# Stores of h and y issued from ScalarE's queue, with a new search of the instruction order

## The chip, the cores and the metric

The kernel runs on one core of a Trainium2 chip. The metric is the device time of one execution in microseconds; of several runs the median is taken. The core's engines work side by side, each through its own list of instructions in order: TensorE (PE; PEld is its weight load) multiplies matrices, VectorE (DVE), ScalarE (ACT) and GpSimd (POOL) work on elements, and SyncE (SP) only issues transfers. Any engine with a queue for transfers can issue one, and it then waits in its own list until the data are ready.

## What is computed

Attention over 32 heads, then two feed-forward layers on the 2304 tokens, all in float32. The names in the code: h is a layer's first product, g what its activation makes of it, y the layer's second product.

```python
def _attn_ref(q, k, v):                       # q, k, v: (4, 8, 576, 64)
    scores = scale * np.matmul(q, k.transpose(0, 1, 3, 2))
    scores = np.where(mask, scores, -1000000000.0)     # causal by blocks of 64
    attn = softmax(scores)
    return np.matmul(attn, v)

def _moe_ref(x, w_in, w_out):                 # x: (2304, 512), d_ff 2048
    h = x @ w_in
    g = np.where(pos, h, np.where(neg, 0.0, (h + beta) ** 2 / (4.0 * beta)))
    return g @ w_out

def _moe2_ref(x, w_in, w_out):
    h = x @ w_in
    g = np.maximum(0.01 * h, h)
    return g @ w_out
```

## The kernel before

**Stages.** Attention by pairs of heads (scores line 651, transposes 743, values 770) runs together with the first layer's first product (lines 877, 887 and 855). Then come the first layer's y (lines 1191 and 1252), the second layer's h (line 1068) and the second layer's y (line 1252 again), whose result is the output. Operands are split into a high and a low part, so that each product is three matmuls.

**Seven products for eight.** From the first layer's y on, each 2x2 block product is made of seven products (`PRODUCTS`), one PSUM bank or pair of banks each. `sums` (line 970 and on) puts them together: ScalarE copies the first product into an SBUF tile (line 978, the copy), and VectorE adds the other six in seven additions (line 976), each of which frees a bank.

**The second layer's h.** `h_step(b, p, ...)` makes one step: 42 matmuls, the sum into a tile of A0 or A1 in turn, the activation in place (Prelu, line 1072, on ScalarE) and one store of 576 KB into the DRAM array `gd[1]` (line 1073). There are 4 parts b of 288 positions with 8 steps p each, 32 steps in all. The copy of a step can only start when the store of the step two before it, from the same tile, has landed.

**y between the layers.** The first layer's y goes to the DRAM array `x2d`: the first 384 positions by `y_group` (stores in `y_out`, line 1124, 4 of 384 KB), the rest in three units of 256 positions by `y_unit` (line 1260, 4 stores of 256 KB each). In a unit each step p loads g (line 1231, `gd`), VectorE makes sums and differences of it (line 1211), ScalarE rounds them to high parts (lines 1236 and 1237, the conversions) and VectorE subtracts for the low parts (1238 and 1240). The second layer's y runs through `y_unit` too and stores to `out` (line 1268, 18 stores, two for the last unit of 128 positions).

**What sets the order.** Nothing is run by hand: the code above only records operations in a `Plan`, each with an engine, a cost in ns and what it reads and writes. `Plan.schedule` then lists them: it simulates the engines with the recorded costs, lists forward and backward in turn, disturbs the keys at random, and keeps the best of `TRIES` lists; `SEED` starts the random numbers. Each engine's instructions are written out in that order. A transfer is an operation of SyncE whose cost is its bytes by a fixed rate (`dma`), with the fixed delays of the table `DELAY` to those that wait for it:

```python
def dma(nbytes, prio, fn, r, w, lag=0):
    plan.op("SP", nbytes / 330.0, prio, fn, r, w, lag=lag)
```

In the first 20 us products of zeros (line 545) are put where the plan leaves TensorE idle. Before the change every transfer of the kernel is SyncE's, 588 in all.

Of the kernel before, what the change touches and what calls it, by code (L numbers as in the profile page):

```python
# [36 lines left out]
HALF = S // 2  # L37
NPOS = B * HALF
# [28 lines left out]

ENTRY = 105
SLACKS = (0, 800)
SEED, TRIES = 6, 400  # L70
LATEST, DRAWS = 0, 1


# [299 lines left out]
def fused_kernel(ctx, tc, qk, v, w1, w2, out):  # L373
    nc = tc.nc
    w1, w2 = w1.bitcast(I32), w2.bitcast(I32)
    plan = Plan()
# [14 lines left out]
    x2d = dr.tile([128, 4, 2, NPOS], F32, tag="x2d", name="x2d")  # L391
    gd = [dr.tile([NP2, 128, 4, NPOS], F32, tag=f"gd{i}", name=f"gd{i}") for i in range(2)]
# [29 lines left out]
    def dma(nbytes, prio, fn, r, w, lag=0):  # L422
        plan.op("SP", nbytes / 330.0, prio, fn, r, w, lag=lag)


    stack = {"ps": [], "ps2": [], "psr": []}

# [628 lines left out]
    def h_step(b, p, pr, dp, banks_):  # L1056
        h = (A1, A0)[p % 2].reg(0, 1152, shape=lambda ap: ap.rearrange("p (s t) -> p s t", s=4))
        P = {}
        for o, m in enumerate(ORDER):
            li, ri = PRODUCTS[m]  # L1060
            r = RX[b, ri]
            ps = bank(banks_[0])
            banks_.append(banks_.pop(0))
            P[m] = ps, lambda ps=ps: ps.get()[:, 0:HALF]
            for k, (cw, cx) in enumerate(((0, 0), (1, 0), (0, 1))):
                def f(k=k, cw=cw, cx=cx, ps=ps, li=li, r=r):
                    for kc in range(2):
                        nc.tensor.matmul(ps.get()[:, 0:HALF], lhsT=wc(1, p, cw, li, 128 * kc, 128 * kc + 128), rhs=r.get()[:, cx, kc],  # L1068
                                         start=(k == 0 and kc == 0), stop=(k == 2 and kc == 1), skip_group_check=True)
                pe(266, pr + dp * o / 7 + 0.01 * k, f, [WC[1, p][cw][li > 2], (r, (cx, cx + 1))], [ps])  # L1070
        sums(pr - 6, HALF, h, P, lambda o: h.get()[:, (1, 3, 0, 2)[o]], ALU.add)
        act(1152, pr - 6, lambda: nc.scalar.activation(h.get(), h.get(), AF.Prelu, alpha=0.01), [h], [h], sb=True)  # L1072
        dma(589824, pr - 6, lambda: nc.sync.dma_start(gd[1][p, :, :, b * HALF:b * HALF + HALF], h.get()), [h],
            [(f"g1{p}", (b * HALF, b * HALF + HALF))])

    HOMES = [{"gr": ([(P1, 1536), (P1, 2560), (P1, 3584)], [(P1, 0), (P1, 1152), (P1, 2304), (P1, 3456)]),
# [44 lines left out]
    def y_out(Y, o, i, prio):  # L1121
        pos0, n = Y["pos"], Y["n"]
        b = Y["bufs"][i]
        dma(1024 * n, prio, lambda: nc.sync.dma_start(x2d[:, o, :, pos0:pos0 + n], b[1]()), [b[0]], [(f"x2d{o}", (pos0, pos0 + n))])

    def y_sums(Y, grp, first, prio, P):
        n, bufs = Y["n"], Y["bufs"]
# [85 lines left out]
    def y_unit(layer, pos0, n, p0, dp, banks_):  # L1213
# [4 lines left out]
        w = n if wide else 256  # L1218
# [37 lines left out]
        if wide:  # L1256
            yo = A0.reg(0, 2048, shape=lambda ap: ap[:, 0:8 * n].rearrange("p (o t n) -> p o t n", o=4, t=2))
            sums(p1, 2 * n, yo, P, lambda o: yo.get()[:, o], ALU.subtract)
            for o in (0, 3, 2, 1):
                dma(1024 * n, p1 + 1, lambda o=o: nc.sync.dma_start(x2d[:, o, :, pos0:pos0 + n], yo.get()[:, o]), [(yo, (o, o + 1))],  # L1260
                    [(f"x2d{o}", (pos0, pos0 + n))])
            return
        yo = A0.reg(0, 2048, shape=lambda ap: ap[:, 0:1024 * nt].rearrange("p (k t i n) -> p k t i n", k=2, t=nt, i=2))
        sums(p1, 256 * nt, yo, P, lambda o: yo.get()[:, o % 2, :, o // 2], ALU.subtract)
        for k in range(2):
            for t in range(nt):
                for a, m, t0, d in runs(pos0 + 128 * t, 128):
                    dma(2048 * m, p1 + 1, lambda k=k, t=t, a=a - pos0 - 128 * t, m=m, r=t0 + k * d: nc.sync.dma_start(
                        out[r:r + m, :].rearrange("q (i n) -> q i n", i=2), yo.get()[a:a + m, k, t]), [(yo, (k, k + 1)), (yo, (2 + k, 3 + k))], [])


# [151 lines left out]
```

## Time and profile before

| what | value |
|---|---|
| median of three runs | 934.44 us |
| the three runs | 928.88, 934.44, 935.6 us |
| the profiled execution's own time | 928.28 us |
| span in its profile | 926.5 us |
| TensorE busy | 915.6 us, 99% |
| VectorE, ScalarE, GpSimd busy | 727.7, 519.6, 293.9 us |
| moved by DMA | 216.72 MB |

The span runs from the first to the last instruction in the profile; the time of the execution has a little around it. A busy share is an average over the stages, and a row of a timeline joins neighbouring instructions of one line: its first number is the start, the second the length, both in us, and a bracket at its end gives the idle time ahead of it and what ended that. Landing times of transfers and the waits of SyncE come from views of their own.

### The profile page before, as it was taken

To read this page: it belongs to the slowest core of one execution; us is meant where nothing else is said; L and a number is where in the kernel's file an instruction comes from. 1 tells how busy PE (TensorE), PEld (TensorE's weight loads), DVE (VectorE), ACT (ScalarE), POOL (GpSimd) and SP (SyncE) were. 2 spreads that over 40 slices of the span, in tenths; PEclk is the share of its full clock that TensorE was granted. 3 is DMA by queue.
4 is the path that set the end of the run, shared out by engine and by line. 5 is a ranking of instruction groups with operands and counts; after the bars stand their busy time and mean duration, and the time that the engine had idled before them with its cause. 6 is when DMAs were issued, how large, how long until landed. Compare 5 with 4: busy or idle time off the path is not lost.

```text
span 926.5 us, 18684 instructions
## 1 busy us (share of the span) xinstructions
PE 915.6 (99%) x6818; PEld 827.7 (89%) x6818; DVE 727.7 (79%) x1247; ACT 519.6 (56%) x1014; POOL 293.9 (32%) x490
## 2 busy tenths in 40 slices
PE   9999999999999999999999999999999999999998
PEld 6687887876777878899999999999999999999998
DVE  6998677777777646559989798677879899888977
ACT  7788677787777666653434343344535664434333
POOL 5577787787665400000000040146445000000000
PEclk9999999999999999999999999999999999999999
DMA  8678788788799789656525499987887983544433
GB/s 310 212 224 249 236 281 285 261 275 272 273 315 323 276 263 325 191 172 209 154 84 161 140 348 337 346 290 269 266 279 242 328 269 91 176 132 139 148 91 115
DMA packets 164892, 216.72 MB, mean 234 GB/s; under 512 B 9920, under 2 KB 138432, under 8 KB 164800
## 3 DMA queue, kind: packets, MB, share of 16 engines
q1 hardware_dynamic: 164800, 215.52, 71.8%
q8 instruction: 54, 0.88, 0.4%
q14 instruction: 38, 0.31, 0.1%
HBM read 134.74 MB, written 80.74 MB: 233 GB/s over the span
## 4 chain that ended last, share of the span: by engine, by line
PE 92%; DVE 2%; DMA 2%; ACT 1%; issue 1%; POOL 1%; SPq 0%; POOLq 0%; DVEq 0%; ACTq 0%
PE bank L1252 31%; PE bank L1068 15%; PE bank L855 14%; PE bank L887 7%; PE bank L1191 6%; PE slot L651 5%; PE slot L770 5%; PE slot L743 5%; DMA rg<-gd 1%; DVE ra L976 1%; DMA wcd<-rg 1%; DMA rb<-x1d 1%; ACT rp L573 1%; PE bank L545 1%; PE slot L762 0%
## 5 line engine op out<-in xcount | busy, mean ns | idle before, releaser
L1068 PE MATMUL bank<-rp,w 128*128 128x288 f32 x1344 | 179.7, 294 | 1.2 <-ACT ra L978 0.9
L1068 PEld LDWEIGHTS bank<-rp,w 128*128 128x128 f32 x1344 | 178.1, 188 | 1.8 <-ACT ra L978 1.2
L976 DVE TENSOR_TENSOR ra<-ra,bank 128x288 f32<-128x288 f32 (+2 forms) x280 | 125.8, 488 | 43.7 <-ACT ra L978 21.8
L1252 PE MATMUL bank<-w,rp 128*128 128x256 f32 x1014 | 145.9, 277 | 0.0
L1252 PEld LDWEIGHTS bank<-w,rp 128*128 128x128 f32 x1014 | 129.8, 188 | 0.0
L855 PE MATMUL bank<-ra,w 128*128 128x512 f32 x384 | 100.0, 398 | 0.3 <-DVE rg L838 0.3
L1237 ACT ACTIVATE rp<-ra 128x1024 fp32r<-128x1024 f32 (+1 forms) x48 | 47.5, 991 | 72.5 <-DVE ra L1211 62.7
L855 PEld LDWEIGHTS bank<-ra,w 128*128 128x128 f32 x384 | 70.1, 188 | 17.1 <-issue 2.3
L838 DVE SCALAR_TENSOR_TENSOR rg<-bank,rg 128x512 f32<-128x512 f32 x72 | 49.3, 684 | 38.0 <-ACT rg L837 35.1
L1072 ACT ACTIVATE ra<-ra 128x1152 f32<-128x1152 f32 x32 | 37.3, 1167 | 71.4 <-DVE ra L976 71.4
L1252 PE MATMUL bank<-rp,w 128*128 128x256 f32 x508 | 76.6, 279 | 0.0
L936 POOL TENSOR_TENSOR w<-w 128x128 f32<-128x128 f32 x128 | 66.9, 543 | 26.7 <-DVE w L932 24.7
L1003 POOL TENSOR_TENSOR xs<-xs,rp 128x576 f32<-128x576 f32 x1 | 1.5, 1547 | 212.0 <-DMA xs<-x2d 212.0
L836 ACT ACTIVATE rg<-bank 128x512 f32<-128x512 f32 x72 | 43.1, 598 | 43.2 <-PE bank L855 36.6
L1252 PEld LDWEIGHTS bank<-rp,w 128*128 128x128 f32 x508 | 67.2, 188 | 0.0
L1240 DVE TENSOR_TENSOR rb<-ra,rp 128x1024 fp32r<-128x1024 f32 (+1 forms) x48 | 54.3, 1133 | 3.9 <-ACT rp L1237 0.7
L1252 PE MATMUL bank<-w,rb 128*128 128x256 f32 x294 | 57.0, 277 | 0.0
L887 PE MATMUL bank<-ra,w 128*128 128x256 f32 x352 | 53.6, 289 | 0.0
L855 PE MATMUL bank<-rb,w 128*128 128x512 f32 x192 | 53.1, 398 | 0.0
L887 PEld LDWEIGHTS bank<-ra,w 128*128 128x128 f32 x352 | 45.1, 188 | 3.5 <-issue 2.6
L1252 PE MATMUL bank<-rg,w 128*128 128x256 f32 x280 | 47.7, 279 | 0.0
L1236 ACT ACTIVATE rp<-rp 128x768 fp32r<-128x768 f32 (+1 forms) x33 | 26.4, 803 | 36.2 <-DMA rp<-gd 21.5
(169 smaller groups left out, 1977.6 us busy)
## 6 DMA issues: line engine op xcount, KB each, us to landing
rp<-gd SPq DMA_DIRECT2D x41, 512.0 KB, 4.2
wcd<-w SPq DMA_DIRECT2D x43, 448.0 KB, 4.6
gd<-ra SPq DMA_DIRECT2D x32, 576.0 KB, 4.8
gd<-rg SPq DMA_DIRECT2D x64, 256.0 KB, 3.6
w<-wcd SPq DMA_DIRECT2D x32, 512.0 KB, 5.7
w<-wcd SPq DMA_DIRECT2D x32, 384.0 KB, 5.7
w<-w SPq DMA_DIRECT2D x44, 256.0 KB, 4.6
w<-w SPq DMA_DIRECT2D x16, 512.0 KB, 5.1
```

The costliest lines, as they stand in the source:

```text
L651: nc.tensor.matmul(out, lhsT=x.get()[r, q:q + 128], rhs=x.get()[r, k0 + ka:k0 + kb], start=start, stop=True, skip_group_check=True)
L743: nc.tensor.transpose(s.get()[:, hd, o:o + 128], prob(hd, a, a + 128), ident.get())
L838: dve(512, pv, lambda: nc.vector.scalar_tensor_tensor(gt.get(), ps.get(), 1.0, gt.get(), op0=ALU.max, op1=ALU.min), [ps, gt], [gt])
L855: nc.tensor.matmul(ps.get(), lhsT=win(fc, c, kc), rhs=xview(xt, x, kc), start=(k == 0 and kc == 0), stop=(k == 2 and kc == NKC - 1), skip_ ...
L887: nc.tensor.matmul(ps.get()[:, 256 - j * 256:512 - j * 256], lhsT=win(fc, c, kc), rhs=xview(xt, x, kc), start=(k == 0 and kc == 0 and j == 0),
L936: plan.op("POOL", 430, prio, lambda o=o, a=a, b=b, op=op: nc.gpsimd.tensor_tensor(sl(o), sl(a), sl(b), op=op), [(fx, (a, a + 1)), (fx, (b, ...
L976: dve(cols, prio, lambda: nc.vector.tensor_tensor(out(o), out(a), P[b][1](), op=op), [P[b][0], (slots, (a, a + 1))], [(slots, (o, o + 1))])
L1068: nc.tensor.matmul(ps.get()[:, 0:HALF], lhsT=wc(1, p, cw, li, 128 * kc, 128 * kc + 128), rhs=r.get()[:, cx, kc], start=(k == 0 and kc == 0 ...
L1191: nc.tensor.matmul(ps[t].get()[:, 0:n], lhsT=wc(z, p, cw, li, 128 * t, 128 * t + 128), rhs=x.get()[:, n * zi:n * zi + n], start=(p == 0 an ...
L1237: act(4 * n, pv, lambda tt=tt, ht=ht: nc.scalar.activation(s_(ht, 0, 4), s_(tt, 0, 4), AF.Copy), [tt], [ht], sb=True)
L1240: dve(4 * n, pv, lambda tt=tt, ht=ht, lt=lt: nc.vector.tensor_tensor(s_(lt, 0, 4), s_(tt, 0, 4), bc(s_(ht, 0, 4)), op=ALU.subtract), [tt, ...
L1252: nc.tensor.matmul(ps.get()[:, 256 * t:256 * t + w], lhsT=b if wide else g, rhs=g if wide else b, start=(p == 0 and k == 0 and t == 0), st ...
```

## The change

Stores of three places, and the second of the last two output stores, are recorded as operations of ScalarE. There the plan counts them with 500 ns of ScalarE's time, and their bytes as a delay behind it instead of as SyncE's time. `SEED` goes from 6 to 1, so the search for the order starts from other random numbers.

```diff
-SEED, TRIES = 6, 400
+SEED, TRIES = 1, 400
...
+    def act_dma(nbytes, prio, fn, r, w):
+        plan.op("ACT", 500, prio, fn, r, w, lag=nbytes / 330.0 + 2300)
+
...
-        dma(589824, pr - 6, lambda: nc.sync.dma_start(gd[1][p, :, :, b * HALF:b * HALF + HALF], h.get()), [h],
+        act_dma(589824, pr - 6, lambda: nc.scalar.dma_start(gd[1][p, :, :, b * HALF:b * HALF + HALF], h.get()), [h],
...
-        dma(1024 * n, prio, lambda: nc.sync.dma_start(x2d[:, o, :, pos0:pos0 + n], b[1]()), [b[0]], [(f"x2d{o}", (pos0, pos0 + n))])
+        act_dma(1024 * n, prio, lambda: nc.scalar.dma_start(x2d[:, o, :, pos0:pos0 + n], b[1]()), [b[0]], [(f"x2d{o}", (pos0, pos0 + n))])
...
-                dma(1024 * n, p1 + 1, lambda o=o: nc.sync.dma_start(x2d[:, o, :, pos0:pos0 + n], yo.get()[:, o]), [(yo, (o, o + 1))],
+                act_dma(1024 * n, p1 + 1, lambda o=o: nc.scalar.dma_start(x2d[:, o, :, pos0:pos0 + n], yo.get()[:, o]), [(yo, (o, o + 1))],
...
+                    put, eng = (act_dma, nc.scalar) if k and pos0 + n == NPOS else (dma, nc.sync)
```

Lines of the new file are three higher than before from line 426 on (four from the output store on), so the copy of line 978 is line 981 there, the Prelu 1075, the store of h 1076, the conversions 1239 and 1240, the y store 1263.

**ScalarE, early in the steps of h.** Copies (978, 981), Prelus in place (1072, 1075) and the splitting of inputs (1007, 1010); ra0 and ra1 are the two tiles of h. First before, then now.

```order
L1072 ACTIVATE ra1_7_6070<-ra1_7_6070 128x1152
L978 ACTIVATE ra0_4_4067<-bank4_90 128x288
L1072 ACTIVATE ra0_4_4067<-ra0_4_4067 128x1152
L978 ACTIVATE ra1_7_6070<-bank1_4043 128x288
L1007 ACTIVATE rp1_2_3911<-ra1_7_6070 128x576
L1072 ACTIVATE ra1_7_6070<-ra1_7_6070 128x1152
```

```order
L1075 ACTIVATE ra0_4_4070<-ra0_4_4070 128x1152
L981 ACTIVATE ra1_7_6090<-bank5_91 128x288
L1076 DMA gd1_71<-ra0_4_4070 512x1x288
L1075 ACTIVATE ra1_7_6090<-ra1_7_6090 128x1152
L1076 DMA gd1_71<-ra1_7_6090 512x1x288
L981 ACTIVATE ra0_4_4070<-bank4_90 128x288
```

The stores, which stood in SyncE's list, now stand in ScalarE's: some behind the next step's copy, as the first one here, some straight ahead of it, as the second.

**ScalarE, at the end of the first y unit.** The copy of the unit's first product (978, 981), the stores into x2d (1263), and the conversions of the next unit's g (1236 and 1237; 1239 and 1240). First before, then now.

```order
L1236 ACTIVATE rp2_2_3954<-rp1_2_3911 128x768
L978 ACTIVATE ra0_4_4067<-bank4_90 128x512
L1237 ACTIVATE rp2_2_3954<-ra1_5_4810 128x1024
L1236 ACTIVATE rp2_2_3954<-rp1_2_3911 128x768
L1237 ACTIVATE rg_2_4729<-ra1_5_4810 128x1024
```

```order
L1240 ACTIVATE rg_2_4728<-ra1_5_4806 128x1024
L981 ACTIVATE ra0_4_4070<-bank4_90 128x512
L1263 DMA x2d_69<-ra0_4_4070 128x2x256
L1239 ACTIVATE rg_2_4728<-rp1_2_3930 128x768
L1263 DMA x2d_69<-ra0_4_4070 128x2x256 x3
L1240 ACTIVATE rp2_2_3966<-ra1_5_4806 128x1024
```

One conversion moved ahead of the copy, and three stores stand together ahead of another.

**ScalarE, in the last steps of h.** The copies of the seventh and of the eighth step of the last part (banks 1 and 0), with weight splits (963, 966) and the first conversions of the last y between them. First before, then now.

```order
L1072 ACTIVATE ra0_4_4067<-ra0_4_4067 128x1152
L1237 ACTIVATE rp2_2_3954<-xs_1_237 128x1024
L978 ACTIVATE ra1_7_6070<-bank1_4043 128x288
L963 ACTIVATE w3_1_565<-w2_1_415 128x1024
L963 ACTIVATE w3_1_565<-w2_1_415 128x768
L1236 ACTIVATE rp2_2_3954<-rb0_20_7623 128x768
L963 ACTIVATE w5_1_781<-w4_1_638 128x1024
L1072 ACTIVATE ra1_7_6070<-ra1_7_6070 128x1152
L978 ACTIVATE ra0_4_4067<-bank0_4042 128x288
```

```order
L981 ACTIVATE ra1_7_6090<-bank1_3988 128x288
L1075 ACTIVATE ra0_4_4070<-ra0_4_4070 128x1152
L1076 DMA gd1_71<-ra0_4_4070 512x1x288
L966 ACTIVATE w3_1_616<-w2_1_460 128x1024
L966 ACTIVATE w3_1_616<-w2_1_460 128x768
L1240 ACTIVATE rp2_2_3966<-xs_1_233 128x1024
L1075 ACTIVATE ra1_7_6090<-ra1_7_6090 128x1152
L1239 ACTIVATE rp2_2_3966<-rb0_20_7613 128x768
L1076 DMA gd1_71<-ra1_7_6090 512x1x288
L981 ACTIVATE ra0_4_4070<-bank0_3987 128x288
```

The copy of the seventh step (bank1) stands ahead of a Prelu now, that of the eighth (bank0) behind a Prelu, a conversion and a store.

## Rows read from the trace of the kernel before

**Rows 1.** The page: busy time of each engine; the costliest conversion line

```profile
PE 915.6 (99%) x6818; PEld 827.7 (89%) x6818; DVE 727.7 (79%) x1247; ACT 519.6 (56%) x1014; POOL 293.9 (32%) x490
...
L1236 ACT ACTIVATE rp<-rp 128x768 fp32r<-128x768 f32 (+1 forms) x33 | 26.4, 803 | 36.2 <-DMA rp<-gd 21.5
```

**Rows 2.** Busy us per stretch: PE, PEld, DVE, ACT, POOL; clock, DMA share, GB/s

```profile
0.00:50.00 50.00, 46.17 (x358) 34.20 (x358) 40.76 (x87) 38.50 (x119) 28.55 (x64) 1.00 0.78 256
50.00:397.00 347.00, 344.77 (x2282) 269.83 (x2281) 246.21 (x435) 253.81 (x617) 194.40 (x331) 1.00 0.83 271
397.00:573.00 176.00, 176.00 (x1342) 175.83 (x1343) 146.88 (x198) 71.88 (x78) 9.64 (x4) 1.00 0.62 196
573.00:752.00 179.00, 177.81 (x1342) 177.17 (x1342) 145.19 (x295) 85.09 (x118) 61.30 (x92) 1.00 0.87 288
752.00:926.50 174.50, 170.89 (x1502) 170.69 (x1500) 148.69 (x236) 70.36 (x84) 0.00 (x0) 1.00 0.45 137
```

**Rows 3.** Waits of PE: us in total, times, longest

```profile
PE bank L545 <- DVE wz L541: 1.1, 1, 1.1
...
PE bank L1068 <- ACT ra L978: 0.9, 1, 0.9
...
PE bank L1068 <- DVE ra L976: 0.3, 1, 0.3
```

**Rows 4.** Timeline of the end, VectorE

```profile
922.93 0.42 DVE L976 TENSOR_TENSOR ra<-ra,bank 128x256 f32<-128x256 f32 x1 [0.40 <-PE bank L1252]
```

**Rows 5.** Issues of lines 1073 and 1260: duration ns min/median/max, first and last start

```profile
L1073 SPq DMA_DIRECT2D gd<-ra x32: 518/519/561, 578.5 to 757.1; - x32
...
L1260 SPq DMA_DIRECT2D x2d<-ra x12: 359/362/1322, 488.1 to 574.2; - x12
```

**Rows 6.** Waits of SyncE: us in total, times, longest

```profile
SPq L1231 <- PE bank L1252: 163.9, 50, 10.2
...
SPq L1073 <- ACT ra L978: 31.7, 15, 4.8
SPq L1073 <- ACT ra L1072: 26.2, 13, 3.3
```

**Rows 7.** Waits of ScalarE and VectorE: us in total, times, longest

```profile
ACT ra L1072 <- DVE ra L976: 71.4, 28, 4.8
ACT rp L1237 <- DVE ra L1211: 62.7, 41, 5.0
...
DVE ra L976 <- ACT ra L978: 21.8, 13, 5.0
```

**Rows 8.** Timeline at the end of the first y unit

```profile
485.92 0.60 ACT L978 ACTIVATE ra<-bank 128x512 f32<-128x512 f32 x1 [1.27 <-PE bank L1252]
486.56 3.49 DVE L976 TENSOR_TENSOR ra<-ra,bank 128x512 f32<-128x512 f32 x5 [0.91 <-ACT ra L978]
...
493.56 1.06 ACT L1237 ACTIVATE rg<-ra 128x1024 fp32r<-128x1024 f32 x1 [2.03 <-DVE ra L1211]
...
495.14 0.36 SPq L1260 DMA_DIRECT2D x2d<-ra  x1
```

**Rows 9.** Timeline of the passage from h to the last y

```profile
745.00 1.06 PE L1068 MATMUL bank<-rp,w 128*128 128x288 f32 x6 [0.92 <-ACT ra L978]
...
750.70 0.39 ACT L978 ACTIVATE ra<-bank 128x288 f32<-128x288 f32 x1
...
752.03 0.86 PE L1252 MATMUL bank<-w,rg 128*128 128x256 f32 x6
```

**Rows 10.** Timeline of PE in attention

```profile
202.30 1.08 PE L855 MATMUL bank<-ra,w 128*128 128x512 f32 x4
203.31 0.81 PE L651 MATMUL slot<-w 64*128 64x320 f32 x4
...
206.42 1.08 PE L855 MATMUL bank<-rb,w 128*128 128x512 f32 x4
207.34 2.13 PE L743 MATMUL slot<-ident,w 128*128 128x128 f32 x18
```

More of the change, by code (lines that the diff above doesn't have):

```diff
@@ L1267, in y_unit @@
                 for a, m, t0, d in runs(pos0 + 128 * t, 128):
-                    dma(2048 * m, p1 + 1, lambda k=k, t=t, a=a - pos0 - 128 * t, m=m, r=t0 + k * d: nc.sync.dma_start(
+                    put, eng = (act_dma, nc.scalar) if k and pos0 + n == NPOS else (dma, nc.sync)
+                    put(2048 * m, p1 + 1, lambda eng=eng, k=k, t=t, a=a - pos0 - 128 * t, m=m, r=t0 + k * d: eng.dma_start(
                         out[r:r + m, :].rearrange("q (i n) -> q i n", i=2), yo.get()[a:a + m, k, t]), [(yo, (k, k + 1)), (yo, (2 + k, 3 + k))], [])
```

## The prediction

> **What bounds the kernel now.** First the page's busy shares: TensorE is busy 915.6 of 926.5 us, VectorE 79%, ScalarE 56% [rows 1]. So whatever the change does, it can only work on the 10.9 us in which TensorE is idle, or make TensorE idle more. Next the busy time by stage shows where those 10.9 us lie, at a granted clock of 1.00 throughout [rows 2]: 50.00 - 46.17 = 3.8 us in the first 50 us, 2.2 us in the rest of attention and of the first product, nothing at all in the 176 us of the first layer's y (397 to 573), 1.2 us in the second layer's h and its passage to the last y (573 to 752), and 3.6 us in the last stretch. Then the list of what TensorE waited for: it has twelve rows, three of which the sum uses [rows 3]. All twelve name ScalarE, VectorE, GpSimd or issue; none names a DMA. That is the first thing to see: the change takes stores off SyncE's queue, and TensorE never waited directly for anything that this queue brought.
>
> Of the 10.9 us some can't go: 1.1 us at the start is the wait for the first zeros [rows 3], and the last 3.6 us are the last sum and its store: the last addition starts at 922.93 us, for it waited for TensorE's last product [rows 4], and the rest up to 926.5 is that addition, a store's issue and its landing. So 10.9 - 1.1 - 3.6 = 6.2 us is all that a perfect order could win.
>
> **The change, part by part.** The profiled execution took 928.28 us (span 926.5 and 1.8 around it); the sum is made against that.
>
> *SyncE loses 49 issues*: 32 stores of h, 12 and 4 of y, 1 of the output. An h store holds SyncE 0.52 us, a y store 0.36 us [rows 5], so about 32 x 0.52 + 17 x 0.36 = 23 us of SyncE's time go. What SyncE did there was mostly to wait: 31.7 + 26.2 us for h, but 163.9 us for TensorE to free the buffers of the gd loads [rows 6]. Loads that stood behind an h store can go earlier now. As no idle time of TensorE ended with a DMA [rows 3], I take 0; the bound on the good side is the 6.2 us above, if loads are what makes ScalarE's conversions, and through them TensorE, late.
>
> The Trainium skill speaks here (DMA: Bandwidth & Descriptors, Issuing engines are not separate DMA queues): transfers issued from different engines share the same 16 DMA engines, so issuing from more of them saves only the sequencer's issue time. By that rule this part is worth at most the 23 us of SyncE, none of it on the path, and the sum stays as it is; were a second queue new bandwidth, the stage at a DMA share of 0.87 [rows 2] would be relieved by it, and rival 2 below would be the likelier.
>
> *ScalarE gains the same 49 issues.* No row shows a DMA issued by ScalarE; SyncE's 0.52 and 0.36 us are the nearest, so ScalarE goes from 519.6 to about 543 us, 59%. In the stretch of h it is busy 85.1 of 179 us [rows 2] and gets 17 more. Its idle time covers that: the Prelu waited 71.4 us in 28 waits for the additions, 2.5 us each, and the y conversions 62.7 us for VectorE [rows 7]. What the mean does not cover is order. In the built order 10 of the 32 stores stand straight between their Prelu and the copy that starts the next step's sum, which comes 0.52 us later there. But VectorE already waited 21.8 us for these copies, in 13 waits [rows 7], and TensorE lost only 0.9 us to it [rows 3]: in this stage late copies are absorbed by the other banks. I take 0; the bound on the bad side is 10 x 0.52 = 5.2 us. If that cover is gone, TensorE waits for the bank of the next step's first product.
>
> *At the ends of the first layer's y units* ScalarE now waits in its queue for VectorE's additions. In the trace of before the copy starts at 485.92 and the last store leaves at 495.14, 9 us later; the conversion that is now queued behind the stores started at 493.56, after an idle 2.03 us [rows 8]. The new VectorE order puts the additions closer: five, which took 3.49 us at 486.56, then a subtraction, an addition, a subtraction of half the columns and the last addition, estimated at a fifth of the 3.49 for the same columns: 3.49 + 3.5 x 0.70 = 5.9 us, from 0.64 us after the copy's start as at 486.56. With the last store's issue the held conversion can start 0.64 + 5.9 + 0.36 = 6.9 us after the copy, against 493.56 - 485.92 = 7.6 us. I take 0, the bounds being 0 and 2 us (as long as the idle time there) for each of the three units, 6 us.
>
> *The passage from h to the last y.* In before TensorE stood idle for 0.92 us until 745.00, for the copy of the seventh step of the last part [rows 9], which ScalarE did only after a Prelu and a conversion, and a little later 0.3 us for an addition [rows 3]; together 1.2 us. In the new order that copy stands ahead of the Prelu: this stall should go. The copy of the eighth step, on the other hand, now stands behind a Prelu, a conversion of 768 columns (0.8 us by the page's own mean for that line [rows 1]) and a store (0.5 us), where before it followed its Prelu directly, so it is 1.3 us later. In before it ended at 750.70 + 0.39 = 751.09, and TensorE next used the bank at 752.03 [rows 9]: a margin of 0.9 us, so 0.4 us of the delay shows. -1.2 + 0.4 = -0.8 us; bounds -1.2, and +1.3 if the margin has gone.
>
> *The order searched anew.* Same products, same number of zero products in the start. But counted in the built order TensorE now goes 61 times from products on the full array into those on part of it (lines 651, 762, 770; three more in the new file), 55 before. One such entry costs 0.09 us: four products of 512 columns followed by line 743 take 207.34 - 206.42 = 0.92 us, followed by line 651 203.31 - 202.30 = 1.01 us [rows 10]. 6 x 0.09 = +0.5 us. The start (2.7 us of idle beside the 1.1) is ordered nearly as before; I take 0 there, between -2.7 and +2.7.
>
> *The last output store* leaves from ScalarE as soon as the addition ends; the unit's other store has left SyncE by then. 0, at best -0.4.
>
> Sum: 928.28 + 0.5 - 0.8 = 928.0 us, for an execution like the profiled one. The executions of before lie at 928.28, 928.88, 934.44 and 935.6; nothing in one trace tells why. Their middle, 931.7, is 3.4 above the profiled one, and a median of new runs can fall in either pair; so 928.0 + 3.4 = **931.4 us**.
>
> **The rivals.**
> 1. *No part of it is felt* (the forecast): 931.4, and anything between 925.1 and 943.8, which is 1% either side of 934.44 and about what a measurement of this kernel can tell from no change.
> 2. *Faster: late loads were behind ScalarE's lateness.* The stores no longer hold up loads on SyncE, and the 6.2 us go: 928.28 + 0.5 - 6.2 = 922.6, or 926.0 with the 3.4. For it: 57.9 us of SyncE's waits are for h stores [rows 6]. Against: 2.7 of the 6.2 us lie in the first 50 us and 2.2 more before 397 us [rows 2], where no store is moved.
> 3. *Slower: ScalarE held at a store.* Place: the three ends of y units, where three stores stand together ahead of a conversion. If the additions come later than the order supposes, that conversion and then TensorE wait. It decides once the last addition is more than the 2.03 us late that ScalarE idled there [rows 8]. Price: the 6 us of the units, and with the 5.2 us of the copies 11.2: 928.0 + 11.2 = 939.2, or 942.6 with the 3.4. For it: VectorE took over 9 us for its additions in before. Against: TensorE had no idle time at all there [rows 2], and ScalarE waits for VectorE anyway.
> 4. *Slower a little: stores and loads now run side by side.* At the stage's 196 GB/s [rows 2] a y store of 256 KB takes 1.3 us of all DMA engines (an estimate from that row); a gd load that ScalarE waits for would land up to that much later, at twelve stores 16 us, of which at a quarter on the path 4: 928.0 + 4 + 3.4 = 935.4. The Trainium skill says (DMA: Bandwidth & Descriptors, Queues, rings and completion order) that a DMA engine takes its queue rows in turn, a packet at a time; by that rule a store no longer queues with the loads but shares with them. No run here shows it yet.
>
> **How the numbers follow.** Chances: forecast 0.62, faster rival 0.15, held ScalarE 0.13, side by side 0.10. The range reaches from 922 (the faster rival without the 3.4) to 941 (most of the held case), about 0.8 of the chance. Faster by over 1% means under 925.1: over half of rival 2 and a little of the forecast, 0.12. Slower by over 1% means over 943.8: a third to half of rival 3, and a start that went badly, 0.10. Within 1%: 0.78.
>
> **What would show it.** Right: TensorE busy within 1 us of 915.6 + 0.5; its idle time between 397 and 573 still under 1 us; ScalarE's issue of an h store near 0.52 us; the stall at about 744 us gone or smaller; ScalarE's wait for the additions shorter by the issue time. Wrong: DMA rows among TensorE's waits (rival 4); rows of lines 1252 or 1068 (1255, 1071 in the new file) with idle time ended by ScalarE's conversions or copies, above all near 490, 530 and 572 us (rival 3); store issues on ScalarE of 1 us and more; or more idle time in the first 50 us, which would be the search's doing and not the stores'.

## The result, and the profile after

The changed kernel takes 941.48 us (median of 12 runs, 936.94 to 949.81) against 928.68 for the kernel before beside it: 1.0144 times as long, 95% interval 1.0118 to 1.0169. It is slower, by more than 1%, and it lies just above the forecast range. The profiled execution took 939.9 us, span 938.0.

The stretches of [rows 2] in the changed kernel (busy us of PE, PEld, DVE, ACT, POOL; granted clock, DMA share, GB/s):

```profile
50.00:397.00 347.00, 346.41 (x2285) 271.22 (x2285) 246.19 (x436) 253.82 (x619) 197.78 (x331) 1.00 0.84 272
397.00:573.00 176.00, 176.00 (x1343) 175.84 (x1342) 147.72 (x198) 71.56 (x76) 7.88 (x4) 1.00 0.62 196
573.00:752.00 179.00, 171.25 (x1265) 168.84 (x1264) 132.09 (x277) 77.55 (x108) 63.16 (x92) 0.99 0.80 269
752.00:938.00 186.00, 180.94 (x1576) 180.06 (x1575) 160.28 (x254) 78.38 (x94) 0.00 (x0) 1.00 0.48 146
```

Up to 573 us nothing is lost; TensorE is busy all of 397:573, so the ends of the y units cost nothing. In 573:752, the second layer's h, it does 1265 matmuls where it did 1342. What TensorE (565 to 790 us), ScalarE (565 to 760) and SyncE (556 to 610) waited for (total us, times, longest), from a list of each:

```profile
PE bank L1071 <- ACT ra L981: 4.2, 5, 1.6
PE bank L1071 <- DVE ra L979: 3.4, 3, 2.0
```
```profile
ACT ra L1075 <- DVE ra L979: 34.0, 22, 4.3
ACT ra L981 <- DMA gd<-ra: 24.8, 10, 4.8
...
ACT ra L981 <- DMA x2d<-ra: 8.1, 1, 8.1
```
```profile
SPq L963 <- DMA gd<-ra: 7.3, 1, 7.3
```

In before the Prelu waited 71.4 us for the additions [rows 7], now 34.0. In its place the copy (L981) waits, 24.8 + 8.1 us, for a store to land. Where it begins, on ScalarE's timeline (start, length, what; brackets: idle ahead and what ended it):

```profile
573.44 0.41 ACT L981 ACTIVATE ra<-bank 128x288 f32<-128x288 f32 x1 [1.41 <-PE bank L1255]
574.30 0.37 ACTq L1263 DMA_DIRECT2D x2d<-ra  x1
581.98 0.41 ACT L981 ACTIVATE ra<-bank 128x288 f32<-128x288 f32 x1 [8.12 <-DMA x2d<-ra]
582.28 1.16 ACT L1075 ACTIVATE ra<-ra 128x1152 f32<-128x1152 f32 x1
583.47 0.59 ACTq L1076 DMA_DIRECT2D gd<-ra  x1
587.65 1.17 ACT L1075 ACTIVATE ra<-ra 128x1152 f32<-128x1152 f32 x1 [4.21 <-DVE ra L979]
591.14 0.41 ACT L981 ACTIVATE ra<-bank 128x288 f32<-128x288 f32 x1 [2.33 <-DMA gd<-ra]
591.23 0.57 ACTq L1076 DMA_DIRECT2D gd<-ra  x1
```

The last y store leaves at 574.30. The copy of the second h step uses its tile and stands in ScalarE's list ahead of the first step's Prelu; it can start at 581.98, so the Prelu waits too, and the first h store leaves at 583.47 (578.5 in before [rows 5]). The third copy waits for that landing until 591.14, and the second store behind it, ready at 588.82, leaves at 591.23. TensorE stops twice, and its granted clock falls after the first stop (columns as above):

```profile
578.00:580.00 2.00, 2.00 (x17) 2.00 (x16) 0.45 (x2) 0.00 (x0) 0.00 (x0) 1.00 1.07 399
580.00:582.00 2.00, 0.96 (x8) 0.73 (x6) 0.00 (x0) 0.02 (x1) 0.00 (x0) 1.00 1.06 388
582.00:584.00 2.00, 1.07 (x4) 1.07 (x5) 0.46 (x1) 1.44 (x2) 0.00 (x0) 0.74 0.99 341
584.00:586.00 2.00, 2.00 (x11) 2.00 (x10) 1.64 (x4) 0.00 (x0) 0.00 (x0) 0.50 0.93 292
586.00:588.00 2.00, 2.00 (x15) 2.00 (x15) 1.00 (x3) 0.35 (x1) 0.65 (x1) 0.90 0.89 271
```

**Where the time is, for all runs.** The h products are 1344 matmuls in every run. The table counts from the trace's matmul records how long their stage takes, from the first of them to the last, in its four parts of eight steps (the first holds some 30 us of y's last products too), and what is left from there to the end of the span. That remainder is near 174.6 us in some traces and near 180 in others whose last stage has the same instructions (before and e12); so the h stage tells more than a median does. Only one execution of each kernel was traced. "Places" are those that the h tiles use in turn.

| kernel | h stores issued by | places | median us | ratio to before (95%) | h stage us: parts, sum | rest |
|---|---|---|---|---|---|---|
| before | SyncE | 2 | 928.68 | | 72.2, 44.4, 44.4, 47.6: 208.7 | 174.6 |
| changed | ScalarE | 2 | 941.48 | 1.0144 (1.0118-1.0169) | 79.0, 45.5, 45.7, 49.0: 219.2 | 175.4 |
| *order of before* | | | | | | |
| e16, y stores alone | SyncE | 2 | 928.82 | 1.0007 (0.9985-1.0029) | 72.5, 44.4, 44.4, 47.6: 209.0 | 174.7 |
| e13, behind the Prelu | ScalarE | 2 | 940.27 | 1.0131 (1.0084-1.0177) | 77.3, 44.4, 46.0, 52.1: 219.8 | 174.6 |
| e14, the same | ScalarE | 3 | 933.55 | 1.0062 (1.0042-1.0083) | 72.3, 44.4, 45.2, 50.3: 212.2 | 180.6 |
| e17, e13 with SyncE's wait | ScalarE | 2 | 933.21 | 1.0038 (1.0014-1.0062) | 72.3, 44.4, 44.9, 52.0: 213.7 | 174.6 |
| e15, behind the next copy | ScalarE | 2 | 934.38 | 1.0073 (1.0045-1.0101) | 78.6, 44.4, 44.4, 47.8: 215.3 | 180.3 |
| e18, the same | ScalarE | 3 | 929.40 | 1.0014 (0.9986-1.0041) | 72.6, 44.4, 44.4, 47.6: 209.1 | 175.9 |
| e9, ScalarE busier | SyncE | 2 | 930.07 | 0.9999 (0.9981-1.0018) | 73.0, 44.4, 44.4, 50.0: 211.8 | 174.4 |
| e12 | SyncE | 3 | 928.68 | 0.9996 (0.9967-1.0026) | 72.2, 44.4, 44.4, 47.6: 208.7 | 180.4 |
| *order of the change* | | | | | | |
| e1, all stores SyncE's | SyncE | 2 | 936.81 | 1.0076 (1.0046-1.0106) | 74.7, 44.4, 45.2, 47.5: 211.8 | 179.6 |
| e2, y stores SyncE's | ScalarE | 2 | 943.31 | 1.0128 (1.0079-1.0177) | 78.3, 44.4, 47.9, 49.9: 220.4 | 181.4 |
| e3, wait by VectorE | ScalarE | 2 | 949.45 | 1.0193 (1.0144-1.0242) | 78.4, 44.4, 50.0, 51.0: 223.9 | 180.4 |
| e4 | ScalarE | 3 | 927.69 | 0.9991 (0.9962-1.0020) | 71.5, 44.4, 44.4, 46.5: 206.9 | 174.5 |
| e5, copies behind stores | ScalarE | 2 | 953.40 | 1.0259 (1.0235-1.0284) | 75.6, 50.6, 48.1, 53.8: 228.1 | 180.0 |
| e10, the same | ScalarE | 3 | 944.57 | 1.0165 (1.0119-1.0212) | 74.1, 49.1, 48.4, 52.1: 223.8 | 180.9 |
| *searched anew* | | | | | | |
| e7, seed 1 | SyncE | 2 | 931.91 | 1.0020 (0.9988-1.0052) | 71.7, 44.4, 45.5, 45.8: 207.4 | 174.7 |
| e8, seed 6 | ScalarE | 2 | 945.67 | 1.0188 (1.0158-1.0217) | 83.7, 45.1, 45.4, 48.0: 222.2 | 178.7 |
| e6, later landing | ScalarE | 2 | 956.37 | 1.0289 (1.0262-1.0317) | 75.0, 45.6, 47.4, 55.9: 224.0 | 179.3 |
| e11, plan knows 3 | ScalarE | 3 | 945.68 | 1.0166 (1.0135-1.0198) | 81.8, 45.7, 44.7, 55.7: 227.9 | 172.7 |

Of the 11.5 us between the two spans (938.0 - 926.5), 219.2 - 208.7 = 10.5 lie in the h stage. TensorE idles there for 8.4 us, 1.2 in before; the clock behind the first stop costs some 1.7 us more, an estimate from the rows above (2 us each at 0.74, 0.50 and 0.90).

### The profile page after: what moved, and what is told of

The parts are those of the page before. It is cut to its first block, busy times and chain, and to the rows that moved or that the text cites. A ratio compares the mean times of both kernels' runs of the same rounds, so it can differ in the third digit from the quotient of the medians.

```text
span 938.0 us, 18643 instructions
## 1 busy us (share of the span) xinstructions
PE 921.1 (98%) x6818; PEld 829.8 (88%) x6818; DVE 725.5 (77%) x1247; ACT 519.6 (55%) x1014; POOL 299.5 (32%) x490
## 4 chain that ended last, share of the span: by engine, by line
PE 87%; DMA 6%; DVE 3%; ACT 2%; issue 1%; ACTq 0%; DVEq 0%
PE bank L1255 30%; PE bank L858 14%; PE bank L1071 12%; PE bank L890 7%; PE bank L1194 6%; PE slot L654 6%; PE slot L773 5%; PE slot L746 5%; DMA gd<-ra 5%; DVE ra L979 1%; DMA x2d<-ra 1%; ACT ra L1075 1%; PE bank L548 1%; ACT rp L576 0%; ACT ra L981 0%
## 5 line engine op out<-in xcount | busy, mean ns | idle before, releaser
L1071 PE MATMUL bank<-rp,w 128*128 128x288 f32 x1344 | 184.1, 296 | 7.8 <-ACT ra L981 4.2
L1255 PE MATMUL bank<-w,rp 128*128 128x256 f32 x1014 | 143.5, 276 | 0.7 <-ACT rp L1239 0.6
L1240 ACT ACTIVATE rp<-ra 128x1024 fp32r<-128x1024 f32 (+1 forms) x48 | 47.5, 990 | 70.5 <-DVE ra L1214 69.4
L939 POOL TENSOR_TENSOR w<-w 128x128 f32<-128x128 f32 x128 | 64.4, 522 | 25.0 <-DVE w L935 22.9
L1255 PE MATMUL bank<-w,rb 128*128 128x256 f32 x294 | 55.1, 276 | 0.0
L981 ACT ACTIVATE ra<-bank 128x288 f32<-128x288 f32 (+2 forms) x40 | 17.6, 439 | 65.9 <-DMA gd<-ra 24.8
L890 PEld LDWEIGHTS bank<-ra,w 128*128 128x128 f32 x352 | 45.7, 188 | 5.8 <-issue 5.4
```

Of the source, the lines that this page charges most:

```text
L890: nc.tensor.matmul(ps.get()[:, 256 - j * 256:512 - j * 256], lhsT=win(fc, c, kc), rhs=xview(xt, x, kc), start=(k == 0 and kc == 0 and j == 0),
L939: plan.op("POOL", 430, prio, lambda o=o, a=a, b=b, op=op: nc.gpsimd.tensor_tensor(sl(o), sl(a), sl(b), op=op), [(fx, (a, a + 1)), (fx, (b, ...
L1240: act(4 * n, pv, lambda tt=tt, ht=ht: nc.scalar.activation(s_(ht, 0, 4), s_(tt, 0, 4), AF.Copy), [tt], [ht], sb=True)
L1255: nc.tensor.matmul(ps.get()[:, 256 * t:256 * t + w], lhsT=b if wide else g, rhs=g if wide else b, start=(p == 0 and k == 0 and t == 0), st ...
```

## The experiments

They are told by question; numbers not shown again stand in the table. The expectations call their theories by letters. A: weight loads run ahead of the stores, and these land late. B: copies that stand ahead in ScalarE's list hold up the Prelu and the store behind them. C: the search drew a worse order (in e3's expectation: a second queue lands late by itself). D: the 0.52 us of a store's issue have no room in the chain of a step.

### Seed or stores?

`SEED` alone, in both kernels:

```diff
-SEED, TRIES = 6, 400      # e7: the kernel before
+SEED, TRIES = 1, 400
-SEED, TRIES = 1, 400      # e8: the changed kernel
+SEED, TRIES = 6, 400
```

> The kernel before (all stores SyncE's) with only the seed of the search changed from 6 to 1, as the change has it. Theory C (the new order is a worse draw of the search, and the queue matters little): 935 to 942. Theories A and B (it takes the moved stores): 927 to 932.

> The changed kernel (stores on ScalarE's queue) with the seed of the kernel before, 6. Theory C: 927 to 932. Theory A (landing on the second queue too late for two tiles): 936 to 943. Theory B allows either: the time goes by how many copies stand ahead of the Prelu or store of the step before, over 936 with ten or more, under 932 with three or fewer.

With SyncE's stores the other seed makes no difference that can be told; with ScalarE's stores both seeds lose. As the whole cause theory C falls: it takes the moved stores. What the order of the change costs without them is e1's question, below.

### Which stores?

In the order of the kernel before, one part alone:

```diff
-            dma(... nc.sync.dma_start(x2d[...], yo.get()[:, o]) ...)      # e16, and y_out
+            dma(... nc.scalar.dma_start(x2d[...], yo.get()[:, o]) ...)
-   act(1152, ..., lambda: nc.scalar.activation(h.get(), ... Prelu))      # e13
+   act(1152, ..., lambda: (nc.scalar.activation(h.get(), ... Prelu), nc.scalar.dma_start(gd[1][...], h.get())))
-   dma(589824, ..., lambda: nc.sync.dma_start(gd[1][...], h.get()), ...)
+   dma(589824, ..., lambda: None, ...)
```

> The kernel before with its own order, and the other part of the change alone: the 16 y stores are issued by ScalarE, the h stores stay with SyncE. Theory A as first put (weight loads run ahead once SyncE doesn't wait for y's data): landings of the last y stores over 6 us, a slip of the first h steps, 932 to 938. If only the h stores cost: 927 to 932.

> The kernel before with its own order, and one part of the change alone: the 32 h stores are issued by ScalarE, each right behind its Prelu. The y stores stay with SyncE. Theory D (the issue of 0.52 us in the chain of a step): 8 to 17 us slower, 937 to 946, the h stage longer in each of its four parts. Theory A (late landings on a second queue with two tiles): slower mainly in the first part, at 574:605, 933 to 940. If neither, the time stays at 927 to 932.

The y stores cost nothing. With the h stores alone moved the kernel takes 940.27 us, as much as with the whole change. Moving only the y stores of the changed kernel back to SyncE agrees:

```diff
-  act_dma(... nc.scalar.dma_start(x2d[...], yo.get()[:, o]) ...)        # e2
+  act_dma(... nc.sync.dma_start(x2d[...], yo.get()[:, o]) ...)
```

> The changed kernel, same order, with only the 12 y stores of the three units (line 1263) issued by SyncE again; the 32 h stores stay with ScalarE. Theory A: the weight loads are held up again while y's last unit ends, the store that landed after 7.58 us lands after 4 to 5, the first slip of some 8 us at 574:582 shrinks to under 5, and the time is 931 to 936, part of the loss. Theory B: no change, 937 to 941.

No gain, though the last y store landed after 5.1 us by the trace, 7.6 in the changed kernel: so theory A was wrong on where it starts.

### Is it the landing?

A third place for the h tiles in turn takes the copy's wait for a landing away. A0 grows by 832 columns for it; the order stays.

```diff
-    (("ra0", 2048), ...
+    (("ra0", 2880), ...
+        own, z = ((A1, 0), (A0, 1728), (A0, 0))[(8 * b + p) % 3]      # in h_step; the view is made from here
```

> The changed kernel, same order and queues, but the h tiles go round three places of SBUF in place of two, so that a copy of line 981 waits for the store of the step three before it, not two, and the second step doesn't use the tile of y's last stores. Landings stay late (6 to 8 us) in every theory. Theories A and B both have the loss pass through the copy's wait for a landing: those waits of ScalarE fall from 33 us to under 5, PE is busy over 24 of the 25 us of 573:598, and the time is 928 to 933. If the loss comes by another way (VectorE's order, ScalarE's issues of 0.52 us each), the time stays at 938 to 942.

> The kernel before, its order and SyncE's stores, with three places for the h tiles in turn at the same instructions. A control: only 6 of its 30 copies start right at a landing, so the third place is worth at most 3 us here if it mends what the change broke (925 to 930); if a third place makes any kernel of this kind some 10 us faster, 916 to 922.

> As the run before it (order of the kernel before, the h stores issued by ScalarE right behind the Prelu), with three places for the h tiles in turn, so that no copy waits for a landing. Theory D: as slow as with two places, 937 to 946. Theory A: 927 to 932.

The changed kernel is back at 927.69. The stretch where it lost most, and the landings of its h stores:

```profile
573.00:598.00 25.00, 25.00 (x191) 25.00 (x190) 17.75 (x38) 8.21 (x12) 6.29 (x10) 1.00 1.06 378
```
```profile
DMA to landing us min/median/max: 3.3/5.3/8.7
```

For the changed kernel with two places the same stretch reads

```profile
573.00:598.00 25.00, 21.45 (x149) 20.98 (x148) 11.98 (x27) 6.27 (x9) 2.61 (x5) 0.93 0.89 308
```

The landings are as late as they were: over all 32 stores 3.3/4.9/7.8 us in the changed kernel, and for the first four 8.27, 6.99, 8.45 and 8.70 us with three places, 7.59, 5.75, 7.85 and 5.49 with two. (Over all 32, before has 3.4/4.8/7.9: its landings are shorter at the start of the stage only.) The control e12 gains nothing: the third place mends what the change broke. So the loss of the changed kernel passes through the copies that wait for a landing. In the order of before, with the store straight behind the Prelu, the third place mends the first part (77.3 to 72.3) and 6.7 us of the time, and 933.55 is left: there is a second cause.

### Why do the stores land late?

In e13 the first four h stores land after 9.78, 6.85, 9.02 and 6.70 us, in before after 4.72, 3.91, 5.48 and 4.80. SyncE's timeline in before, then in e13, there with ScalarE's row of the store:

```profile
575.61 0.41 SPq L960 DMA_DIRECT2D w<-wcd  x1
576.08 0.49 SPq L957 DMA_DIRECT2D w<-wcd  x1
578.48 0.56 SPq L1073 DMA_DIRECT2D gd<-ra  x1
579.13 0.58 SPq L960 DMA_DIRECT2D w<-wcd  x1
```
```profile
575.13 0.42 SPq L960 DMA_DIRECT2D w<-wcd  x1
575.62 0.49 SPq L957 DMA_DIRECT2D w<-wcd  x1
576.20 0.42 SPq L960 DMA_DIRECT2D w<-wcd  x1
576.67 1.50 SPq L957 DMA_DIRECT2D w<-wcd  x3
577.60 0.62 ACTq L1072 DMA_DIRECT2D gd<-ra  x1
578.22 0.53 SPq L960 DMA_DIRECT2D w<-wcd  x1
```

In before SyncE stood at the store until the Prelu was done, and that held back the weight loads behind it: two had left since 575. In e13 nothing holds them: five have left since 575 by the time the store goes at 577.60, and two follow at once. To give SyncE its wait back and leave the store on ScalarE's queue:

```diff
+   (..., nc.scalar.dma_start(gd[1][...], h.get()), nc.scalar.activation(tk[one element], ...))      # e17, behind the Prelu
-   dma(589824, ..., lambda: nc.sync.dma_start(gd[1][...], h.get()), ...)
+   dma(589824, ..., lambda: nc.sync.dma_start(tkd[...], tk[one element]), ...)
```

> The kernel before with its own order and the h stores issued by ScalarE right behind the Prelu, two places for the h tiles, as in the run at 940.3; but at the place where each store stood in SyncE's list SyncE issues a transfer of 4 bytes that ScalarE has written behind the store (some 0.2 us of ScalarE more a step), so that SyncE's loads behind it wait as they did before. If the landings are late because SyncE no longer waits there and its loads run ahead of the store (nine transfers at 572:579 for six before): the first four h stores land after 4 to 6 us in place of 6.7 to 9.8, the first part of the h stage takes 72 to 74 us in place of 77.3, and the time is 931 to 936. If the second queue by itself lands late: landings of 7 to 10 us, a first part of 77 us and 939 to 945.

```profile
575.07 0.43 SPq L963 DMA_DIRECT2D w<-wcd  x1
575.56 0.62 SPq L960 DMA_DIRECT2D w<-wcd  x1
579.00 0.30 SPq L1076 DMA_DIRECT2D tkd<-tk  x1
579.40 0.38 SPq L963 DMA_DIRECT2D w<-wcd  x1
```

The first part takes 72.3 us again, with two places and the stores on ScalarE's queue, and in its list of waits no copy waits for an h store any more. This trace has no landings of the moved stores, but it has their packets, 512 to a store. What the queues moved in the 4.0 us from the issue of the first h store (q1 carries SyncE's transfers, q10 ScalarE's; packets, MB, share of the DMA engines), in e13 (577.60:581.60), which has no row of q10, and in e17 (578.15:582.15):

```profile
q1 hardware_dynamic: 847, 1.43, 100.2%
```
```profile
q1 hardware_dynamic: 428, 0.77, 60.3%
q10 hardware_dynamic: 501, 0.56, 42.1%
```

In e13 the store hadn't begun to move 4 us after its issue; in e17 it was nearly through. So it is SyncE's wait that kept the landings short, not its queue. That is shown in the order of before. In the changed kernel the rows are alike (in 583.47:587.47, from the issue of its first h store, q1 moved 1018 packets and q10 4), and e1 (below), which gives SyncE the wait and the stores back, shortens the first part from 79.0 to 74.7 us; but no run that can be read gave it the wait alone there. An earlier try had VectorE write the element, in the order of the change:

```diff
+   nc.vector.memset(tk[:, i:i + 1], 0.0); nc.sync.dma_start(tkd[...], tk[...])      # e3, behind each y and h store
```

> The changed kernel, same order, stores still on ScalarE's queue; SyncE gets back the wait alone: behind each of the 12 y stores of line 1263 and the 32 h stores of line 1076 VectorE sets one element (some 60 ns each) and SyncE issues a transfer of 4 bytes of it, so that SyncE's loads behind can't start earlier than when the store's data are ready. Theory A (it is the loads that run ahead): the landings fall to 4 to 5.5 us and the time to 929 to 934. Theory B (ScalarE's list), and theory C (a second queue makes the stores land late by itself): landings stay at 6 to 8 us in 574:605 and the time is 938 to 942.

It failed, and it settles nothing: ScalarE waited for that VectorE instruction itself (16.5 us at the Prelu), and only e5 is slower in that order.

### The second cause: what stands where in ScalarE's list

> The kernel before with its own order, the 32 h stores issued by ScalarE at the place where the order has them, which in 27 of 31 steps is behind the copy of the next step: Prelu, next copy, store. The copy waits there for the landing of the store before. Theory D (issue in the chain): no loss by the issue, since it stands behind the copy, so 928 to 934. Theory B (a copy that waits for a landing holds up the store behind it, so that landings push each other on): 938 to 955, worse than with the store right behind the Prelu.

> The kernel before with its own order, the h stores issued by ScalarE behind the copy of the next step, and three places for the h tiles: neither a landing in the way of a copy nor an issue between Prelu and copy. If these two are the whole loss: 927 to 931, an h stage of 207 to 210 us. If carrying the h stores on ScalarE costs by another way too: 933 or more, as with two places.

e15 only exchanges `nc.sync` for `nc.scalar` in the h store; in most steps the list then reads Prelu, next copy, store. e18 adds the three places. Behind the copy the issue costs nothing: parts 2 to 4 are those of before, and with three places so is the first, 929.40. Straight behind the Prelu (e14) a copy that comes next starts 0.65 us after the Prelu's end in most steps, 0.60 at the least, and the last two parts take 0.8 and 2.7 us more. Two more tests of this price:

```diff
+   nc.scalar.activation(busy, zeros, AF.Copy)      # e9: kernel before, behind each Prelu, 512 columns
```
```diff
-        done = best[0]
+        done = self.relist(best[0])      # e5: each h copy behind the store of the step before; e10: and three places
```

> The kernel before, its order and SyncE's stores as they are, with one more instruction on ScalarE behind each of the 32 Prelus: a copy of 512 columns of zeros to a place that nothing reads, some 0.52 us, the time that an h store takes to issue. No transfer changes its queue. Theory D (the chain of a step, copy of line 978, seven additions, Prelu, and in ScalarE's list the copy of the next step, leaves no room for 0.52 us beside TensorE's 5.67 us a step): 938 to 953, with TensorE waiting on the additions (VectorE's line 976) in all of 573:760. Theory A (only late landings of stores on the second queue cost time): 928 to 932.

> The changed kernel with stores on ScalarE's queue and two h tiles as they are, but no copy of line 981 of an h step stands ahead of the Prelu or the store of the step before it in ScalarE's list any more: each that did is put right behind that store, all else keeps its order as far as that allows. Theory B (head of the line: a copy that waits for a landing holds up the Prelu and the store behind it, which makes the next landing later still): the first h store leaves at 579 to 580 instead of 583.5, PE is busy over 24 of the 25 us of 573:598, and the time is 927 to 932. Theory A (the landings of 5.5 to 8.5 us are by themselves too long for two tiles in turn, whatever the order of the list): the time stays at 936 to 941.

> The changed kernel with both edits: every copy behind the store of the step before in ScalarE's list, and three places for the h tiles in turn. No copy should wait for a landing any more. Theory D: the 0.52 us of each store's issue still stands between the Prelu and the next copy, so 943 to 953, near the 953 with two tiles. Theory A: 927 to 932, as with three places and the list as it was.

e9's extra instruction took 0.61 us and the copy came 0.4 us after the Prelu's end; the time is the same within the interval. So theory D in its simple form, no room at all, is wrong. But e9 isn't free: its traced execution, the slowest of its ten, has an h stage 3.1 us longer than before's, and 2.4 of them lie in the last part, as 2.7 of e14's 3.5 do. TensorE stopped there for 1.6 us, where it had stopped for 0.9 in before [rows 3], and its granted clock was then 0.50 (in 750:752; 1.00 in before). So in the order of before the price is small and falls mostly in the last eight steps; whether e9 and e14 differ by the 0.4 and 0.65 us isn't shown. In the order of the change, found with the copies ahead, the price is large: between e4 and e10 the copies' place in ScalarE's list differs, and with it that of seven of VectorE's instructions among the additions, and the h stage grows by 223.8 - 206.9 = 16.9 us, 0.55 a step over 31. That another order of VectorE's other work would make it smaller there is likely by e14, but wasn't tried. As the whole cause theory B falls with e5: there a copy behind the store is worse than one that waits for a landing.

### Leave it to the search?

```diff
-        plan.op("ACT", 500, prio, fn, r, w, lag=nbytes / 330.0 + 2300)      # e6
+        plan.op("ACT", 500, prio, fn, r, w, lag=nbytes / 330.0 + 5500)
```
```diff
-        h = (A1, A0)[p % 2].reg(0, 1152, ...)      # e11
+        own, z = ((A1, 0), (A0, 1728), (A0, 0))[(8 * b + p) % 3]
+        h = own.reg(z, 1152, ...)
```

> The changed kernel with one number of the plan changed: a store on ScalarE's queue is counted to land 3.2 us later than before (5500 for 2300 ns beside its bytes), which is near the 7.6 us seen in 574:605; the order is searched anew from the same seed. If the fault is that the plan took the landings for early and put copies ahead of what they hold up (theory B), the search keeps clear of it: 927 to 933, with fewer copies ahead of the Prelu of the step before than the 11 of 31. If landings are too long for two tiles (theory A): 936 or more whatever the order.

> The changed kernel with three places for the h tiles known to the plan, so that the search may put a copy ahead of the Prelu and store of the step before without a landing in its way. If the two ways of losing (issue in the chain, or landing in the way of a copy put ahead) are all there is, it is as fast as the kernel before or faster: 922 to 930.

Both expectations failed. Told of later landings, the search puts every copy behind the store, as e5 does, and the kernel is as slow. Told of three places, it puts 27 of 31 copies ahead of the Prelu of the step before (11 in the changed kernel, none in before), and the stores go still later. The chain of waits of e11 in 570:602:

```profile
576.22 9.70 DMA x2d<-ra
585.91 0.02 issue
585.94 0.02 ACTq L1077
585.95 0.04 issue
585.99 8.61 DMA gd<-ra
```

The first h store there waits for the last y store to land. The instruction lists say why: in the built program every transfer, whichever engine issues it, takes the next of eight semaphores in turn, and waits until the transfer that had it before has landed. ScalarE's list in e11 (the bracket names the semaphores waited for):

```
651 L1264 DMA x2d<-ra_4_4083 128x2x256 [waits DMAHW5_49,DVE_49]
654 L1077 DMA gd_71<-ra_7_6076 512x1x288 [waits DMAHW5_49,Activation_49]
```

So a late landing also holds whoever issues the transfer eight further on: in the changed kernel SyncE stood 7.3 us for the first h store (its row above), and the load it held there is the eighth transfer behind that store.

### All stores SyncE's again, in the order of the change

```diff
-  nc.scalar.dma_start(...)      # e1: in each moved store, 49 in all
+  nc.sync.dma_start(...)
```

> The changed kernel with every instruction in the same order on PE, DVE, ACT and POOL, but with its 50 moved stores issued by SyncE again, each at the place in SyncE's list where the plan has it. SyncE then waits for a store's data again before it goes on to the weight loads behind it. Theory A (SyncE was freed: weight loads of lines 960 and 963 run ahead from 562 us on, fill the DMA engines, and the last y stores and first h stores land after 5.7 to 7.9 us; the copy of line 981 two steps later waits for that landing): stores land after 4 to 5.5 us, the waits of ScalarE on a landing fall from 33 us to under 8, the granted clock of 573:598 is 1.0, and the time is 928 to 932. Theory B (the new order itself is at fault: copies stand in ScalarE's list ahead of the Prelu and the store of the step before and hold them up, whatever queue carries the stores): the waits stay and the time is 937 to 941.

Between the two: the h stage is 3.1 us longer than before, not 10.5 (a copy that stands ahead of the Prelu still waits for landings, of 8.4 us at most). Another 5.0 us of the profiled execution lie in the last stage, at its slower pace (below), which the kernel before's executions have too by their times, so they aren't put down to the order.

## Why the prediction was wrong

**SyncE loses 49 issues: "I take 0", bound on the good side only.** This is the step that failed. It saw that loads behind an h store could go earlier, and asked only what that wins. SyncE's wait at the h stores (57.9 us in all [rows 6]) was what kept the weight loads from crowding them at the start of the stage. Without it the loads go first, the first four stores land 2 to 5 us later (e13), and the copies wait for that; with the wait given back (e17) they don't. Price in the first part: 77.3 - 72.3 = 5.0 us in the order of before; in the changed kernel the first part grew by 6.8 us and the h stage by 10.5, and three places take all of it away (e4).

**ScalarE gains 49 issues: 0, at worst 5.2 us.** The issue time was right (32 of 520 to 594 ns, the y stores of the units 366 to 380), and in the order that was built the issue costs nothing (e4), as it does behind the copy in the order of before (e15, e18). Straight behind the Prelu it costs 0.4 to 0.6% there (e14, e17), and far more in the order of the change (e10). What was left out is the other thing that a store's place decides: when it lands. The copy two steps later waits for that, a sentence in the description of the kernel that no term took up. That late copies are "absorbed by the other banks" was read from waits of at most 5.0 us [rows 7]; a copy 8.12 us late was not.

**The ends of the y units: 0; the last output store: 0.** Right: TensorE is busy 176.00 of 176.00 us, and e16 is at 928.82; what is left behind the h stage is 174.5 us in e4 for 174.6.

**The passage: -0.8 us; the order anew: +0.5 us.** The second is too small to be told: e7 is at 1.0020 (0.9988 to 1.0052). The first can't be read in the changed kernel, where TensorE comes to the passage some 10 us late. But e4 has the same order without the slip: its last part takes 46.5 us for 47.6, and TensorE's waits in the h stage are 0.5 us for 1.2. That is near the forecast.

**Rivals.** Held ScalarE (3) had the right engine and the wrong place, a copy in the h stage in place of a store at the end of y; that its price of 11.2 us is nearly the loss is luck. Its sign came, idle time of line 1071 ended by copies (4.2 us). Side by side (4) had the right kind, late landings, on the wrong transfers: it feared for the gd loads, and TensorE has no DMA row among its waits now either. Faster (2) had the sign of the freed SyncE wrong.

**The 3.4 us for the executions' spread.** It was mis-sized: nine of twelve executions of before lie at 927.5 to 928.9 us, so their median is 0.4 above the profiled one. Without it the forecast would have been 928.0, and farther off. The two levels of before are most likely the two paces of the last stage: e12 was traced in an execution of 933.89 us and has 180.4 us there, for 174.6 in before's of 928.28.

Open: why no search found an order as good as that of before or e4 with the stores on ScalarE. The plan counts a landing by its bytes and a fixed delay, neither the load on the DMA engines nor the eight semaphores; that this is the reason was not tested. No version here beats the kernel before by more than can be measured: e4 is at 0.9991 (0.9962 to 1.0020).

## What to carry to other kernels

An issuing engine that waits is also a brake on everything behind it in its list; before a transfer is moved off it, ask which transfers will now run ahead, and who waits for the moved one to land. Where two buffers in turn are reused after a store, the loop runs through the landing: a third place took it out here (e4) and cost no time (e12), only 832 columns of SBUF, while the place of the issue in the other engine's list (behind the work that the next step waits for) decides whether the issue is free.

## What the runs showed of the hardware

A store on a queue of its own did not pass the loads issued ahead of it. In e13 the first h store left at 577.60 behind five weight loads (since 575). What the queues (q1 SyncE's, q10 ScalarE's) moved in 577.6:581.9, then in 583:586 (packets, MB, share):

```profile
q1 hardware_dynamic: 910, 1.52, 99.8%
q10 hardware_dynamic: 4, 0.00, 0.3%
```
```profile
q1 hardware_dynamic: 433, 0.71, 63.1%
q10 hardware_dynamic: 405, 0.46, 42.4%
```

For some 4 us the store hardly began; then both queues moved about as many packets, and it landed at 587.38. The Trainium skill (DMA: Bandwidth & Descriptors, Queues, rings and completion order) says that a DMA engine takes its queue rows in turn, a packet at a time. The second stretch agrees with that, 405 packets to 433, if the rule's packets are the trace's; the first shows no turns, and what the store waited for in it was not found. The Trainium skill (the same page, Issuing engines are not separate DMA queues) says that transfers run on the same 16 DMA engines whichever engine issued them; the rates agree, for the second queue brought no more of it: 327 GB/s in 573:598 before, 308 after.

TensorE idled for 1.97 us up to 582.93, and its granted clock was then 0.50, the 1.2 GHz level, through 584:586 before it was 1.00 again at 588. Behind its next stop, 1.58 us up to 591.61, the clock stayed at 1.00.

The last stage ran at one of two paces at a granted clock of 1.00, with TensorE busy throughout 800:820 and the same instructions. First the kernel before, then e12:

```profile
800.00:820.00 20.00, 20.00 (x179) 20.00 (x178) 16.62 (x25) 8.41 (x10) 0.00 (x0) 1.00 0.44 128
```
```profile
800.00:820.00 20.00, 20.00 (x173) 20.00 (x172) 15.77 (x22) 8.38 (x9) 0.00 (x0) 1.00 0.36 107
```

179 matmuls in 20 us or 173, 111.7 or 115.6 ns each, which over the stage is the 5 to 6 us between remainders of 174.6 and 180. What sets it was not found.
